# The first product of an MLP reads its tokens 32 columns apart, and rows of x and results move in one transfer a chunk

## The chip, the cores and the metric

The kernel runs on one core of one Trainium2 chip. A core has a matrix engine (TensorE, PE in the profile; its weight loads are shown as PEld), VectorE (DVE), ScalarE (ACT), GpSimd (POOL) and SyncE (SP), which here only issues DMA transfers. The engines run side by side, each through its own list of instructions in order, and wait for each other by semaphores. SBUF is the working memory with 128 partitions; PSUM takes the products of PE; DRAM holds inputs, outputs and a scratch copy of some rows. The metric is the time of one execution in microseconds on the device.

## What is computed

A linear attention whose features are products of two random projections, and behind it a layer norm with an MLP and a residual:

```python
def phi(x):                       # x: (4, 4, 1088, 32), S1, S2: (8, 32)
    a = np.einsum('rd,bhsd->bhsr', S1, x)
    b = np.einsum('rd,bhsd->bhsr', S2, x)
    return np.einsum('bhsi,bhsj->bhsij', a, b).reshape(*x.shape[:-1], 64)
q_p, k_p = (phi(q), phi(k))
kv = np.einsum('bhsf,bhsd->bhfd', k_p, v)
z = np.sum(k_p, axis=2)
num = np.einsum('bhsf,bhfd->bhsd', q_p, kv)
den = np.einsum('bhsf,bhf->bhs', q_p, z)[..., None] + 1e-06
x = (num / den)                   # then (B, S, H*D) = (4, 1088, 128)
xn = (x - mean(x)) / np.sqrt(var(x) + 1e-06) * g_ln
ch = np.maximum(xn @ w_ch1, 0.0) @ w_ch2     # 128 -> 512 -> 128
out = x + ch
```

All arithmetic is in float32. The MLP weights come as 64 bit floats and are turned into float32 on the chip.

## The kernel before

**Tokens and chunks.** Each of the four batches has 1088 tokens, 32 runs of 34: on loading, partition 32 h + i holds tokens 34 i to 34 i + 33 of head h. The MLP works on ten chunks: chunks 0 to 7 are half a batch, 512 tokens in four tiles of 128, and chunks 8 and 9 hold the remaining 64 tokens of two batches each, one tile of 128. The output of the attention stands in `xT`: features on the 128 partitions, tokens along the columns. `num_cp` copies it there from four PSUM banks, so that column 128 t + 32 r + i of a chunk (tile t, bank r) is token 34 i + 4 r + t of its batch, and 16 more in the second half. The four r of one i, sixteen neighbouring tokens with their four t, lie 32 columns apart.

**The MLP of a chunk.** The layer norm is folded into the products: the mean is taken out by the weights `w1`, and the factor 1/sqrt(var) is applied to the result, since it is positive and passes through the ReLU. `hid` is the first product: for each of four column blocks j of `w1`, the block is the weight and the 512 columns of `xT` are streamed past it, into one PSUM bank. `relu` moves that bank to `hT` in SBUF, on ACT or DVE. `sec` is the second product: for each tile t, the 128 columns of `hT` of that tile are the weights and `w2` streams past, four times, added up in PSUM. So the tokens come out on partitions, in the order in which `hid` read the columns. `fin` (DVE) or `fin_a` (ACT) with `fin_g` (POOL) scale the result and add the row of `x`; `store` writes it to DRAM.

**Rows of x.** The residual and the statistics (`st_bn`, `st_ag` on DVE, `st_pow` on POOL) need `x` with tokens on partitions, in the same order. Chunks 0, 8 and 9 get it by a transposition on PE (`row_pe`, `row_cp`). Chunks 1 to 7 go through DRAM: `row_turn` transposes blocks of 32 x 32 on DVE into `xh`, `row_wr` writes `xh` to the scratch `xd`, and `row_rd` reads it back in another arrangement, in one transfer for each r: 32 partitions, 64 KB. `store` likewise writes 32 partitions (`g` is r there), 64 KB, four times a chunk.

**Order of the work.** Nothing plans the order at run time or build time. `PROGRAM`, a text at the end of the kernel, lists all steps in one order, and each engine gets its instructions in that order; a step's letter S, A, V or G names the engine (SP, ACT, DVE, POOL) that does it, or that issues its DMA. So a transfer issued by ACT stands in ACT's list between its copies and ReLUs, and what it waits for holds up what is behind it. `fill` steps in the early part are products of ones with no use for the result.

The lines that the prediction speaks of: L232, L223, L193 are fills of constants on POOL; L382 is `sk_0`; L553 is `k_sccp` and L652 `q_den`, two reductions on DVE; L787 `row_pe`; L77 a copy on ACT; L802 `row_wr`, L808 `row_rd`; L843 `hid`, L851 `relu` on ACT, L859 `sec`; L872 `fin`, L888 `fin_g`; L893 `store`, L902 `store_r`.

Of the kernel before, what the change touches and what calls it, by code (L numbers as in the profile page):

```python
# [24 lines left out]
def kernel(  # L25
# [32 lines left out]
    dve, act, pool, pe, sp = nc.vector, nc.scalar, nc.gpsimd, nc.tensor, nc.sync  # L58
    by = {"V": dve, "A": act, "G": pool, "S": sp}
# [271 lines left out]
    w1 = const([P, DH], F32, "w1")  # L331
# [435 lines left out]
    xd = [dram.tile([P, 512 if i < 8 else P], F32, name=f"xd{i}") for i in range(10)]  # L767
# [69 lines left out]
    def ob(c):  # L837
        return obs[order.index(c) % len(obs)]

    @op  # L840
    def hid(z, c, j, t0, t1):
        a, n = P * t0, P * (t1 - t0)
        pe.matmul(banks[z][:, 0:n], w1[:, P * j : P * (j + 1)], cols(c)[:, a : a + n], start=True,  # L843
                  stop=True)

    @op
# [41 lines left out]
        by[eng].tensor_tensor(out=o, in0=o, in1=i, op=ALU.add)  # L888

    @op  # L890
    def store(eng, c, g, t0, t1):
        b, half = divmod(c, 2)
        by[eng].dma_start(  # L893
            out=bass.AP(out.tensor, out.offset + (b * S + 16 * half + 4 * g + t0) * DM,
                        [[G * DM, 32], [1, DM * (t1 - t0)]]),
            in_=ob(c)[32 * g : 32 * g + 32, DM * t0 : DM * t1],
        )

    @op
# [50 lines left out]
    k_sccp V 2; relu A C 1 2 0 4; k_val 1; k_tok 3 0 0 9; k_tok 3 1 0 9; row_rd S 1 3; q_turn 0 4;  # L950
    ld_v S 2 0; k_sum 3; q_feat 2 0 9; ld_v S 3 2; k_vcp A 1; sk_qq 3; row_rd S 1 1; st_ag 0;
    k_spr 1; q_tok 2 1 0 9; sec M 0 2; ld_v S 2 2; k_rcp A 1; q_tok 2 2 0 9; ld_v S 3 3;
    q_tok 2 0 0 9; sec O 1 2; row_rd S 1 2; q_tok 2 3 0 9; ld_v S 3 1; k_zs 3; sec M 0 3;
    q_turn 4 9; q_ac G 2 4 9; ld_vr S 3 1; st_pow 0; sec O 1 0; k_prod V 2 0 5; k_prod G 2 5 9;
    k_sc 3; fin_a M 0; num 1 0 9; sec O 1 3; num_cp A 1 1 0 4; num_cp V 1 2 4 8; num_cp A 1 3 0 4;
    num_cp V 1 2 0 4; num_cp A 1 0 0 4; row_rd A 1 0; k_sccp V 3; row_turn 2; hid N 2 3 0 4;
    num_cp A 1 3 4 8; num_r A 1; turn_h q 3 0; row_wr S 2; row_pe 8 D; hid K 2 1 0 4;
    relu A N 2 3 0 4; q_den 2 4 9; turn_h q 3 1; num_cp A 1 0 4 8; hid C 2 2 0 4; q_rec 2 4 9;
    relu A K 2 1 0 4; turn_r q 3; q_ac V 2 0 4; q_a2 G 2 4 9; row_cp A 8 D; q_den 2 0 4;
    num_cp A 1 1 4 8; sec O 1 1; relu A C 2 2 0 4; q_prod V 2 4 9; hid B 3 0 0 4; q_rec 2 0 4;  # L960
# [6 lines left out]
    st_bn 8; sec M 2 0; hid N 3 2 0 4; relu A D 8 3 0 1; relu V K 8 1 0 1; row_rd A 2 1;
    q_ac V 3 4 9; st_ag 1; relu A C 8 0 0 1; k_val 3; row_rd A 2 2; relu V A 8 2 0 1; st_pow 1;
    relu V N 3 2 0 4; q_den 3 4 9; num 2 0 9; q_rec 3 4 9; k_vcp A 3; fin_a O 1; q_a2 G 3 4 9;
    q_ac G 3 0 4; q_prod G 3 4 9; k_spr 3; num_cp V 2 1 4 8; sec O 3 2; num_cp V 2 3 4 8;  # L970
    num_cp V 2 2 0 4; num_cp A 2 3 0 4; st_ag 8; st_bn 3; num_cp A 2 2 4 8; sec O 3 0; k_rcp A 3;
    num_r V 2; sec N 8 0; st_ag 3; num_cp A 2 1 0 4; num_cp V 2 0 0 4; st_pow 3; num_cp V 2 0 4 8;
    hid C 4 2 0 4; row_turn 5; row_turn 4; row_wr S 5; sec O 3 3; fin_g G 1; q_turn 4 9;
    row_wr S 4; sec O 3 1; store S 0 0 0 4; st_bn 2; hid A 5 1 0 4; relu A C 4 2 0 4; row_rd A 5 3;
    q_den 3 0 4; hid C 4 0 0 4; row_rd S 4 1; q_rec 3 0 4; store A 0 1 0 4; relu V A 5 1 0 4;
    store S 0 2 0 4; store A 0 3 0 4; hid D 5 3 0 4; st_ag 2; row_rd S 5 2; fin_a O 3;
    q_a2 V 3 0 4; st_pow 2; store S 1 3 0 4; q_prod V 3 0 4; hid B 4 3 0 4; row_rd S 5 0;
    relu A C 4 0 0 4; hid A 4 1 0 4; relu A D 5 3 0 4; st_pow 8; q_turn 0 4; row_rd S 5 1;
# [6 lines left out]
    num_cp V 3 0 0 4; row_wr A 7; row_cp V 9 N; sec K 5 3; row_turn 6; store A 3 0 0 4;
    row_rd A 4 0; st_bn 5; sec K 4 0; store A 1 1 0 4; st_ag 5; sec K 4 2; row_rd S 7 0; st_pow 5;
    row_wr S 6; hid N 6 2 0 4; st_bn 4; hid B 6 0 0 4; relu A N 6 2 0 4; st_ag 4; store A 2 3 0 4;
    hid C 6 1 0 4; st_pow 4; relu A B 6 0 0 4; row_rd S 6 2; store_r A 8 1; hid A 6 3 0 4;
    relu V C 6 1 0 4; row_rd S 6 1; fin K 4 0; sec N 5 0; row_rd S 6 0; fin D 4 3; row_rd S 7 3;
    sec M 5 2; row_rd S 7 1; fin N 5 0; fin O 4 1; row_rd S 7 2; st_bn 9; row_rd A 6 3;  # L990
    hid C 7 3 0 4; st_ag 9; fin K 4 2; relu V A 6 3 0 4; sec B 5 1; fin M 5 2; sec N 6 0;
    relu A C 7 3 0 4; sec O 6 1; relu V D 9 0 0 1; fin B 5 1; fin K 5 3; hid A 9 2 0 1; st_bn 6;
    store S 5 3 0 4; hid D 7 2 0 4; relu A A 9 2 0 1; store S 4 0 0 4; relu V M 9 3 0 1;
    hid K 7 0 0 4; store S 5 1 0 4; st_ag 6; relu A D 7 2 0 4; st_bn 7; st_pow 6; store_r S 8 0;
    store A 5 0 0 4; hid B 7 1 0 4; store S 3 3 0 4; relu A K 7 0 0 4; st_ag 7; store S 4 2 0 4;
    store A 4 1 0 4; sec D 6 3; st_pow 9; store S 3 1 0 4; store A 4 3 0 4; relu A B 7 1 0 4;
    sec A 6 2; st_pow 7; relu A O 9 1 0 1; fin N 6 0; sec A 7 0; fin O 6 1; fin D 6 3; sec C 7 3;
# [38 lines left out]
```

## Time and profile before

| | us |
|---|---|
| median of three timed runs | 103.03 |
| lowest and highest of them | 102.94, 105.31 |
| the profiled execution, its own time | 102.81 |
| span of the profiled execution | 100.9 |

The span runs from the first to the last event of the profile; the execution's own time also takes in what lies around it.

The page of the profile has the span in 40 equal slices, each digit the busy share of one slice in tenths. In most slices PE is above nine tenths, while DVE, ACT and POOL come and go:

```profile
PE   5988999999999999999999999999999999999960
DVE  2878989789999599699089549999559079661630
ACT  2863754979700720755513353029640030253000
POOL 7115998999588926912999189809920540057000
DMA  2989999893008760030023220346146445054242
```

In rows of groups, a line such as L843 is followed by the engine, the operation, what it writes and reads, the shapes, the count, the busy time in all and the mean of one, and then the idle time of the engine before these instructions with what ended it. In the chain of waits, each step is what released the next one, back from the last instruction; "x2" counts records. A float32 product on PE shows as two records, one for each pass.

### The profile page before, as it was taken

How to read it: one execution, taken by the hardware profiler on the slowest of the kernel's cores; microseconds unless marked ns; L12 is line 12 of the kernel's file. 1: busy time of each engine (PE TensorE's matmuls, PEld its weight loads, DVE VectorE, ACT ScalarE, POOL GpSimd, SP SyncE). 2: the span in 40 equal slices, each digit the busy share in tenths (PEclk: the TensorE clock that was granted, in tenths of full speed). 3: DMA queues.
4: the chain of work that ended last, by engine and by line, in shares of the span. 5: the costliest groups of instructions: out<-in, count | busy, mean ns of one | idle time of the engine just before them, and what ended most of it. 6: DMA issues, size and time to landing. Idle time of an engine off the chain costs nothing.

```text
span 100.9 us, 3433 instructions
## 1 busy us (share of the span) xinstructions
PE 95.3 (94%) x1355; PEld 68.7 (68%) x1355; DVE 74.0 (73%) x239; ACT 41.3 (41%) x119; POOL 58.4 (58%) x83
## 2 busy tenths in 40 slices
PE   5988999999999999999999999999999999999960
PEld 5765668656656779656588669854469758959950
DVE  2878989789999599699089549999559079661630
ACT  2863754979700720755513353029640030253000
POOL 7115998999588926912999189809920540057000
PEclk9999999999999999999999999999999999999999
DMA  2989999893008760030023220346146445054242
GB/s 76 272 293 389 353 370 275 272 218 88 3 6 301 212 164 3 6 130 0 6 107 106 47 59 0 109 153 187 55 107 204 143 122 148 1 115 132 77 119 64
DMA packets 12367, 13.85 MB, mean 137 GB/s; under 512 B 2880, under 2 KB 8768, under 8 KB 12352
## 3 DMA queue, kind: packets, MB, share of 16 engines
q1 hardware_dynamic: 9968, 11.67, 38.8%
q10 hardware_dynamic: 2384, 1.97, 6.7%
q8 instruction: 10, 0.16, 0.7%
q14 instruction: 5, 0.04, 0.2%
HBM read 9.57 MB, written 4.06 MB: 135 GB/s over the span
## 4 chain that ended last, share of the span: by engine, by line
PE 78%; DMA 5%; POOL 5%; DVE 2%; ACT 2%; SPq 2%; issue 1%; ACTq 0%; POOLq 0%
PE bankO L859 8%; PE bankM L859 8%; DMA w_raw<-in_moe_w_ch_dram 5%; PE bankN L843 5%; PE bankK L560 5%; PE bankC L843 4%; PE bankK L843 4%; PE bankK L859 4%; PE bankB L843 3%; PE bankA L843 3%; PE bankD L843 3%; PE bankM L250 3%; PE bankA L859 3%; PE bankN L859 3%; POOL ob L888 2%; PE bankA L735 2%
## 5 line engine op out<-in xcount | busy, mean ns | idle before, releaser
L82 POOL TENSOR_TENSOR kp<-kf 128x1024 f32<-128x1024 f32 (+4 forms) x9 | 15.9, 1779 | 0.1
L827 POOL TENSOR_SCALAR va<-mv 128x4 f32<-128x4 f32 (+1 forms) x10 | 2.3, 228 | 18.2 <-DVE mv L822 17.7
L82 POOL TENSOR_TENSOR qp<-a,fq 128x1280 f32<-128x1280 f32 (+1 forms) x5 | 11.1, 2219 | 0.2
L859 PEld LDWEIGHTS bankO<-w,hT 128*128 128x128 f32 x80 | 9.7, 192 | 1.9 <-issue 1.9
L829 POOL TENSOR_TENSOR rstd<-va,mhalf 128x4 f32<-128x4 f32 (+1 forms) x10 | 10.3, 1034 | 0.8
L859 PE MATMUL bankO<-w,hT 128*128 128x128 f32 x80 | 10.4, 277 | 0.0
L859 PEld LDWEIGHTS bankM<-w,hT 128*128 128x128 f32 x72 | 9.0, 192 | 1.9 <-issue 1.9
L677 DVE STREAM_TRANSPOSE qpT<-qp 128x1280 f32<-128x1280 f32 (+1 forms) x7 | 9.6, 1365 | 0.0
L250 PE MATMUL bankM<-ones 128*128 128x256 f32 (+1 forms) x28 | 8.3, 440 | 1.2 <-DVE top L180 1.2
L859 PE MATMUL bankM<-w,hT 128*128 128x128 f32 x72 | 9.3, 275 | 0.0
L816 DVE BATCH_NORM_STATS2 st<-x 128x6 f32<-128x128 f32 x32 | 6.7, 272 | 2.5 <-issue 2.5
L250 PEld LDWEIGHTS bankM<-ones 128*128 128x128 f32 x28 | 5.7, 241 | 2.5 <-DVE top L180 1.2
L851 ACT ACTIVATE hT<-bankC 128x512 f32<-128x512 f32 (+1 forms) x6 | 3.3, 551 | 8.3 <-PE bankB L859 4.7
L843 PE MATMUL bankC<-xT,w 128*128 128x512 f32 x12 | 6.1, 592 | 0.0
L843 PE MATMUL bankN<-xT,w 128*128 128x512 f32 (+1 forms) x14 | 6.1, 516 | 0.0
L851 ACT ACTIVATE hT<-bankN 128x256 f32<-128x256 f32 (+1 forms) x6 | 3.0, 498 | 7.2 <-PE bankN L843 7.2
L82 POOL TENSOR_TENSOR a<-fq,rden 128x160 f32<-128x160 f32 (+1 forms) x6 | 2.8, 463 | 5.2 <-DVE rden L659 4.8
L560 PEld LDWEIGHTS bankK<-kp,vn 128*32 128x32 f32 x288 | 4.2, 110 | 2.3 <-issue 1.1
L851 ACT ACTIVATE hT<-bankK 128x512 f32<-128x512 f32 (+1 forms) x6 | 3.1, 522 | 6.2 <-PE bankK L843 5.3
L457 DVE STREAM_TRANSPOSE qT<-qn 128x512 f32<-128x512 f32 x8 | 5.5, 687 | 0.0
L843 PE MATMUL bankK<-xT,w 128*128 128x512 f32 (+1 forms) x12 | 5.4, 530 | 0.0
L735 PE MATMUL bankD<-qpT,kvr 32*32 32x288 f32 (+1 forms) x64 | 5.2, 386 | 0.0
(235 smaller groups left out, 255.2 us busy)
## 6 DMA issues: line engine op xcount, KB each, us to landing
kn<-in_k_dram SPq DMA_DIRECT2D x3, 544.0 KB, 6.2
qn<-in_q_dram SPq DMA_DIRECT2D x3, 544.0 KB, 6.4
vn<-in_v_dram SPq DMA_DIRECT2D x12, 128.0 KB, 4.5
xd<-xh SPq DMA_DIRECT2D x5, 256.0 KB, 2.6
x<-xd SPq DMA_DIRECT2D x20, 64.0 KB, 2.0
out_dram<-ob SPq DMA_DIRECT2D x19, 64.0 KB, 1.7
out_dram<-ob ACTq DMA_DIRECT2D x13, 64.0 KB, 1.9
w_raw<-in_moe_w_ch_dram SPq DMA_DIRECT2D x2, 256.0 KB, 4.0
```

The source lines that it names most:

```text
L82: by[eng].tensor_tensor(out=o, in0=a, in1=b, op=ALU.mult)
L250: pe.matmul(M[0][:, 0:w], ones[:, 0:P], ones[:, 0:w], start=True, stop=True)
L457: dve.transpose(_ap(dst[b % 2], 0, P, P * 4 * half, [[32, 4], [P, 4], [1, 32]]), src[b][:, 512 * half : 512 * half + 512],)
L560: pe.matmul(KV[D * h : D * h + D, 0:F], vn[b][:, TW * h + D * u : TW * h + D * (u + 1)], kp[:, H * F * u + F * h : H * F * u + F * (h + 1) ...
L677: dve.transpose(_ap(qpT, 0, P, 32 * u0, [[32, u1 - u0], [TW, 8], [1, 32]]), qp[:, H * F * u0 : H * F * u1])
L735: pe.matmul(X[r][D * h : D * h + D, o : o + w], kvr[b % 2][rows, DM * f + D * h : DM * f + D * h + D], qpT[rows, c : c + w], start=(f == 0 ...
L816: dve.bn_stats(out=sts[slot(c)][:, 6 * t : 6 * t + 6], in_=row_ap(c, t))
L827: pool.tensor_scalar(out=vas[slot(c)][:, 0:n], in0=_ap(mvs[slot(c)], 0, P, 1, [[2, n]]), scalar1=1e-6, scalar2=None, op0=ALU.add)
L829: pool.tensor_tensor(out=rstds[slot(c)][:, 0:n], in0=vas[slot(c)][:, 0:n], in1=mhalf[:, 0:n], op=ALU.pow)
L843: pe.matmul(banks[z][:, 0:n], w1[:, P * j : P * (j + 1)], cols(c)[:, a : a + n], start=True, stop=True)
L851: act.activation(o, i, AF.Relu)
L859: pe.matmul(banks[z][:, DM * t : DM * (t + 1)], h[:, 512 * j + P * t : 512 * j + P * (t + 1)], w2[:, DM * j : DM * (j + 1)], start=(j == 0 ...
```

## The change

`hid` reads the columns of chunks 1 to 7 in another order: within each tile of 128 it takes the columns 0, 32, 64, 96, then 1, 33, 65, 97, and so on, by an access pattern with a step of 32 floats. Since the tokens come out of `sec` in that order, the four r of one i lie on four neighbouring partitions. `row_rd` then reads a chunk's rows with one pattern over 128 partitions, and `store` can write a chunk with one transfer. Chunk 0, whose rows come by PE, keeps its order and its four stores.

```diff
+    woven_chunks = set(range(1, 8))
...
     @op
     def row_rd(eng, c, r):
         w = D * tiles(c)
-        by[eng].dma_start(
-            out=_ap(rows_of(c), 32 * r, 32, 0, [[w, H], [1, w]]),
-            in_=bass.AP(xd[c].tensor, xd[c].offset + w * r, [[P // 32 * w, 32], [P * w, H], [1, w]]),
-        )
+        dst, src = _ap(rows_of(c), 0, P, 0, [[w, H], [1, w]]), [[w, P], [P * w, H], [1, w]]
+        if c > 7:
+            dst = _ap(rows_of(c), 32 * r, 32, 0, [[w, H], [1, w]])
+            src = [[P // 32 * w, 32]] + src[1:]
+        by[eng].dma_start(out=dst, in_=bass.AP(xd[c].tensor, xd[c].offset + w * r, src))
...
+    def woven(y, c, o, t0, t1):
+        if c not in woven_chunks:
+            return y[:, o + P * t0 : o + P * t1]
+        return _ap(y, 0, P, o + P * t0, [[P, t1 - t0], [1, 32], [32, 4]][t1 - t0 == 1 :])
+
     @op
     def hid(z, c, j, t0, t1):
-        a, n = P * t0, P * (t1 - t0)
-        pe.matmul(banks[z][:, 0:n], w1[:, P * j : P * (j + 1)], cols(c)[:, a : a + n], start=True,
+        n = P * (t1 - t0)
+        pe.matmul(banks[z][:, 0:n], w1[:, P * j : P * (j + 1)], woven(cols(c), c, 0, t0, t1), start=True,
                   stop=True)
...
-    def store(eng, c, g, t0, t1):
+    def store(eng, c, t0, t1, g=None):
         b, half = divmod(c, 2)
+        if g is not None:
+            by[eng].dma_start(
+                out=bass.AP(out.tensor, out.offset + (b * S + 16 * half + 4 * g + t0) * DM,
+                            [[G * DM, 32], [1, DM * (t1 - t0)]]),
+                in_=ob(c)[32 * g : 32 * g + 32, DM * t0 : DM * t1],
+            )
+            return
         by[eng].dma_start(
-            out=bass.AP(out.tensor, out.offset + (b * S + 16 * half + 4 * g + t0) * DM,
-                        [[G * DM, 32], [1, DM * (t1 - t0)]]),
-            in_=ob(c)[32 * g : 32 * g + 32, DM * t0 : DM * t1],
+            out=bass.AP(out.tensor, out.offset + (b * S + 16 * half + t0) * DM,
+                        [[G * DM, 32], [4 * DM, 4], [1, DM * (t1 - t0)]]),
+            in_=ob(c)[:, DM * t0 : DM * t1],
         )
```

In `PROGRAM` the four `row_rd` of a chunk become one, at the place of the first, issued by SP for all chunks; the four `store` of chunks 1 to 5 become one, at the place of the first, on SP; chunks 6 and 7 are stored in two halves of two tiles each, one by SP and one by ACT. The four stores of chunk 0 are all on SP. The step `sk_0`, whose result no step reads, is left out. All other steps stay in their order. Some places of it:

```diff
-    q_dir 0 4 O; q_tok 0 0 4 9; sk_0; q_tok 0 3 4 9; ld_vr S 1 1; q_tok 0 2 4 9; c_vpad 2;
+    q_dir 0 4 O; q_tok 0 0 4 9; q_tok 0 3 4 9; ld_vr S 1 1; q_tok 0 2 4 9; c_vpad 2;
...
-    row_rd A 2 3; sec M 2 1; q_tok 3 1 0 9; q_tok 3 2 0 9; k_prod G 3 5 9; hid K 8 1 0 1;
-    hid B 3 3 0 4; q_turn 4 9; k_rcp A 2; row_rd S 3 3; row_rd A 3 2; sec M 2 2; row_rd S 3 1;
+    k_spr 2; q_tok 3 0 0 9; row_rd S 2 0; sec M 2 1; q_tok 3 1 0 9; q_tok 3 2 0 9; k_prod G 3 5 9;
+    hid K 8 1 0 1; hid B 3 3 0 4; q_turn 4 9; k_rcp A 2; row_rd S 3 0; sec M 2 2; relu A B 3 3 0 4;
...
-    hid K 5 0 0 4; relu V O 5 2 0 4; fin_g G 2; store A 3 2 0 4; num 3 0 9; relu A K 5 0 0 4;
-    store S 2 2 0 4; store A 2 1 0 4; store S 1 0 0 4; sec O 4 1; num_cp A 3 3 0 4;
+    fin_g G 2; store S 3 0 4; num 3 0 9; relu A K 5 0 0 4; store S 2 0 4; sec O 4 1;
+    num_cp A 3 3 0 4; num_cp V 3 1 0 4; num_r A 3; fin N 8 0; num_cp A 3 3 4 8; num_cp A 3 1 4 8;
...
-    fin A 6 2; fin A 7 0; store S 6 2 0 4; store A 6 1 0 4; sec B 7 1; store S 6 3 0 4; fin C 7 3;
-    store S 6 0 0 4; sec K 7 2; store S 5 2 0 4; fin B 7 1; sec A 9 0; fin K 7 2; store S 7 0 0 4;
-    store A 7 2 0 4; store S 7 1 0 4; store A 7 3 0 4; fin A 9 0; store_r S 9 0; store_r A 9 1;
+    sec A 7 0; fin O 6 1; fin D 6 3; sec C 7 3; fin A 6 2; fin A 7 0; store S 6 0 2; store A 6 2 4;
+    sec B 7 1; fin C 7 3; sec K 7 2; fin B 7 1; sec A 9 0; fin K 7 2; store S 7 0 2; store A 7 2 4;
+    fin A 9 0; store_r S 9 0; store_r A 9 1;
```

More of the change, by code (lines that the diff above doesn't have):

```diff
@@ L949 @@
     turn_h q 2 1; relu A D 1 0 0 4; k_sc 2; k_feat 3 0 9; relu A N 0 3 2 4; q_prod G 1 4 9;
[L950 to L960, printed above, removed]
@@ L967 @@
[L967 to L978, printed above, removed]
@@ L985 @@
[L985 to L996, printed above, removed]
@@ L997 @@
-    sec A 6 2; st_pow 7; relu A O 9 1 0 1; fin N 6 0; sec A 7 0; fin O 6 1; fin D 6 3; sec C 7 3;
-    fin A 6 2; fin A 7 0; store S 6 2 0 4; store A 6 1 0 4; sec B 7 1; store S 6 3 0 4; fin C 7 3;
-    store S 6 0 0 4; sec K 7 2; store S 5 2 0 4; fin B 7 1; sec A 9 0; fin K 7 2; store S 7 0 0 4;
-    store A 7 2 0 4; store S 7 1 0 4; store A 7 3 0 4; fin A 9 0; store_r S 9 0; store_r A 9 1;
+    k_sccp V 2; relu A C 1 2 0 4; k_val 1; k_tok 3 0 0 9; k_tok 3 1 0 9; row_rd S 1 0; q_turn 0 4;
+    ld_v S 2 0; k_sum 3; q_feat 2 0 9; ld_v S 3 2; k_vcp A 1; sk_qq 3; st_ag 0; k_spr 1;
@@ new lines @@
+    q_tok 2 1 0 9; sec M 0 2; ld_v S 2 2; k_rcp A 1; q_tok 2 2 0 9; ld_v S 3 3; q_tok 2 0 0 9;
+    sec O 1 2; q_tok 2 3 0 9; ld_v S 3 1; k_zs 3; sec M 0 3; q_turn 4 9; q_ac G 2 4 9; ld_vr S 3 1;
+    st_pow 0; sec O 1 0; k_prod V 2 0 5; k_prod G 2 5 9; k_sc 3; fin_a M 0; num 1 0 9; sec O 1 3;
+    num_cp A 1 1 0 4; num_cp V 1 2 4 8; num_cp A 1 3 0 4; num_cp V 1 2 0 4; num_cp A 1 0 0 4;
+    k_sccp V 3; row_turn 2; hid N 2 3 0 4; num_cp A 1 3 4 8; num_r A 1; turn_h q 3 0; row_wr S 2;
+    row_pe 8 D; hid K 2 1 0 4; relu A N 2 3 0 4; q_den 2 4 9; turn_h q 3 1; num_cp A 1 0 4 8;
@@ new lines @@
+    hid C 2 2 0 4; q_rec 2 4 9; relu A K 2 1 0 4; turn_r q 3; q_ac V 2 0 4; q_a2 G 2 4 9;
+    row_cp A 8 D; q_den 2 0 4; num_cp A 1 1 4 8; sec O 1 1; relu A C 2 2 0 4; q_prod V 2 4 9;
+    hid B 3 0 0 4; q_rec 2 0 4; hid A 2 0 0 4; row_turn 3; relu A B 3 0 0 4; q_a2 G 2 0 4;
+    q_prod G 2 0 4; k_val 2; relu A A 2 0 0 4; q_feat 3 0 9; k_vcp A 2; row_wr A 3; fin_g G 0;
+    k_spr 2; q_tok 3 0 0 9; row_rd S 2 0; sec M 2 1; q_tok 3 1 0 9; q_tok 3 2 0 9; k_prod G 3 5 9;
+    hid K 8 1 0 1; hid B 3 3 0 4; q_turn 4 9; k_rcp A 2; row_rd S 3 0; sec M 2 2; relu A B 3 3 0 4;
@@ new lines @@
+    q_tok 3 3 0 9; k_prod G 3 0 5; hid A 8 2 0 1; q_turn 0 4; hid C 8 0 0 1; hid D 8 3 0 1;
+    hid N 3 1 0 4; st_bn 1; sec M 2 3; relu A N 3 1 0 4; st_bn 8; sec M 2 0; hid N 3 2 0 4;
+    relu A D 8 3 0 1; relu V K 8 1 0 1; q_ac V 3 4 9; st_ag 1; relu A C 8 0 0 1; k_val 3;
+    relu V A 8 2 0 1; st_pow 1; relu V N 3 2 0 4; q_den 3 4 9; num 2 0 9; q_rec 3 4 9; k_vcp A 3;
+    fin_a O 1; q_a2 G 3 4 9; q_ac G 3 0 4; q_prod G 3 4 9; k_spr 3; num_cp V 2 1 4 8; sec O 3 2;
+    num_cp V 2 3 4 8; num_cp V 2 2 0 4; num_cp A 2 3 0 4; st_ag 8; st_bn 3; num_cp A 2 2 4 8;
@@ new lines @@
+    sec O 3 0; k_rcp A 3; num_r V 2; sec N 8 0; st_ag 3; num_cp A 2 1 0 4; num_cp V 2 0 0 4;
+    st_pow 3; num_cp V 2 0 4 8; hid C 4 2 0 4; row_turn 5; row_turn 4; row_wr S 5; sec O 3 3;
+    fin_g G 1; q_turn 4 9; row_wr S 4; sec O 3 1; store S 0 0 4 0; st_bn 2; hid A 5 1 0 4;
+    relu A C 4 2 0 4; row_rd S 5 0; q_den 3 0 4; hid C 4 0 0 4; row_rd S 4 0; q_rec 3 0 4;
+    store S 0 0 4 1; relu V A 5 1 0 4; store S 0 0 4 2; store S 0 0 4 3; hid D 5 3 0 4; st_ag 2;
+    fin_a O 3; q_a2 V 3 0 4; st_pow 2; store S 1 0 4; q_prod V 3 0 4; hid B 4 3 0 4;
@@ new lines @@
+    relu A C 4 0 0 4; hid A 4 1 0 4; relu A D 5 3 0 4; st_pow 8; q_turn 0 4; fin_a M 2;
+    hid O 5 2 0 4; fin_g G 3; relu V A 4 1 0 4; relu A B 4 3 0 4; hid K 5 0 0 4; relu V O 5 2 0 4;
+    fin_g G 2; store S 3 0 4; num 3 0 9; relu A K 5 0 0 4; store S 2 0 4; sec O 4 1;
+    num_cp A 3 3 0 4; num_cp V 3 1 0 4; num_r A 3; fin N 8 0; num_cp A 3 3 4 8; num_cp A 3 1 4 8;
+    num_cp V 3 2 0 4; num_cp V 3 2 4 8; hid D 9 0 0 1; hid M 9 3 0 1; num_cp V 3 0 4 8;
+    hid O 9 1 0 1; row_turn 7; row_pe 9 N; sec D 4 3; num_cp V 3 0 0 4; row_wr A 7; row_cp V 9 N;
@@ new lines @@
+    sec K 5 3; row_turn 6; st_bn 5; sec K 4 0; st_ag 5; sec K 4 2; row_rd S 7 0; st_pow 5;
+    row_wr S 6; hid N 6 2 0 4; st_bn 4; hid B 6 0 0 4; relu A N 6 2 0 4; st_ag 4; hid C 6 1 0 4;
+    st_pow 4; relu A B 6 0 0 4; row_rd S 6 0; store_r A 8 1; hid A 6 3 0 4; relu V C 6 1 0 4;
+    fin K 4 0; sec N 5 0; fin D 4 3; sec M 5 2; fin N 5 0; fin O 4 1; st_bn 9; hid C 7 3 0 4;
+    st_ag 9; fin K 4 2; relu V A 6 3 0 4; sec B 5 1; fin M 5 2; sec N 6 0; relu A C 7 3 0 4;
+    sec O 6 1; relu V D 9 0 0 1; fin B 5 1; fin K 5 3; hid A 9 2 0 1; st_bn 6; store S 5 0 4;
@@ new lines @@
+    hid D 7 2 0 4; relu A A 9 2 0 1; store S 4 0 4; relu V M 9 3 0 1; hid K 7 0 0 4; st_ag 6;
+    relu A D 7 2 0 4; st_bn 7; st_pow 6; store_r S 8 0; hid B 7 1 0 4; relu A K 7 0 0 4; st_ag 7;
+    sec D 6 3; st_pow 9; relu A B 7 1 0 4; sec A 6 2; st_pow 7; relu A O 9 1 0 1; fin N 6 0;
+    sec A 7 0; fin O 6 1; fin D 6 3; sec C 7 3; fin A 6 2; fin A 7 0; store S 6 0 2; store A 6 2 4;
+    sec B 7 1; fin C 7 3; sec K 7 2; fin B 7 1; sec A 9 0; fin K 7 2; store S 7 0 2; store A 7 2 4;
+    fin A 9 0; store_r S 9 0; store_r A 9 1;
```

8 lines of the change are left out of this document (removed).

## The prediction

> **What bounds the kernel now.** I read the busy totals first, then the chain of waits, then a table of the busy time by stages whose edges I took from that chain.
>
> ```profile
> span 100.9 us, 3433 instructions
> PE 95.3 (94%) x1355; PEld 68.7 (68%) x1355; DVE 74.0 (73%) x239; ACT 41.3 (41%) x119; POOL 58.4 (58%) x83
> ```
>
> TensorE (PE) is busy for 95.3 of 100.9 us and no other engine for more than 74.0. The table by stages tells whether the rest is spread or sits at the ends (columns after the stage: its length, then PE, PEld, DVE, ACT and POOL busy, granted clock, DMA share, GB/s):
>
> ```profile
> 0.00:8.85 8.85, 6.98 (x106) 5.19 (x106) 5.60 (x29) 4.43 (x11) 2.97 (x20) 1.00 0.74 235
> 8.85:74.54 65.69, 65.58 (x1096) 45.02 (x1096) 54.46 (x149) 32.36 (x98) 49.54 (x54) 1.00 0.44 133
> 74.54:74.93 0.39, 0.27 (x3) 0.08 (x1) 0.28 (x2) 0.39 (x4) 0.00 (x0) 1.00 0.67 137
> 74.93:97.40 22.47, 22.43 (x153) 18.41 (x153) 13.31 (x62) 4.15 (x9) 5.87 (x10) 1.00 0.43 118
> 97.40:100.90 3.50, 0.00 (x0) 0.00 (x0) 0.35 (x1) 0.00 (x0) 0.00 (x0) 0.92 0.37 94
> ```
>
> There are three parts: 8.85 us of loading, 88.55 us in which PE hardly pauses at full granted clock, and 3.50 us after its last product (the last output is finished, stored and lands). Busy could hide waiting, since the ends of matmuls are modelled, so I checked the pace in the chain of waits (start, length, what):
>
> ```profile
> 79.55 0.86 PE bankN L843 x2
> 80.41 0.86 PE bankB L843 x2
> 81.27 0.86 PE bankC L843 x2
> 82.13 0.86 PE bankA L843 x2
> 82.98 0.89 PE bankN L859 x8
> ...
> 97.40 0.35 DVE ob L872
> ```
>
> L843 is `hid`, the first product of the MLP; each call is two matmul records, 0.86 us for 512 columns, so 0.43 us a pass or 0.84 ns a column. Four calls of one chunk follow each other without a gap, and `sec` (L859) follows at once. So a cost or saving on PE goes one to one into the time, and a saving elsewhere only counts where PE waits for it.
>
> **The product read in steps.** For chunks 1 to 7 `hid` now reads the columns of `xT` in the order 0, 32, 64, 96, 1, 33 and so on: four bytes taken, 128 bytes on, where before they were adjacent. That is 7 chunks x 4 calls = 28 calls and 56 passes; chunk 0 (calls of 256 columns) and the remainder chunks 8 and 9 read as before. No PE row of this trace has such a step, so the price needs bounds from the nearest rows. One is GpSimd (POOL), which fills a tile of 36 elements at a step of 9 floats, 36 bytes, and other tiles without a step (last columns: busy in all, mean ns of one):
>
> ```profile
> L232 POOL MEMSET ac<- 128x36 f32 x2 | 0.3, 158 | 0.3 <-POOLq L1020 0.3
> L223 POOL MEMSET kT<- 128x64 f32 x2 | 0.3, 144 | 0.0
> L193 POOL MEMSET ident<- 128x128 f32 x1 | 0.2, 203 | 0.0
> L1020 POOL MEMSET const-float32-1.0<- 128x1 f32 x1 | 0.1, 98 | 0.0
> ```
>
> One element takes 98 ns, which I take as the fixed part. Contiguous elements then cost (203 - 98) / 128 = 0.82 ns or (144 - 98) / 64 = 0.72 ns; the stepped ones (158 - 98) / 36 = 1.67 ns, 2.0 to 2.3 times as much. And 0.82 ns is about the pace at which `hid` reads its columns. This row is in SBUF, where `xT` lies, but it writes, and on another engine. The other neighbour reads: VectorE (DVE) reduces 32 elements out of PSUM four at a time at a step of 8 floats, beside contiguous reductions from SBUF:
>
> ```profile
> L553 DVE TENSOR_REDUCE skq<-bankK 128x8 f32<-128x32 f32 x4 | 0.7, 180 | 0.5 <-PE bankK L545 0.5
> L652 DVE TENSOR_REDUCE den<-ac 128x16 f32<-128x144 f32 x4 | 1.2, 296 | 0.1
> L652 DVE TENSOR_REDUCE den<-ac 128x20 f32<-128x180 f32 x4 | 1.3, 317 | 0.0
> ```
>
> At 0.58 ns an element between the contiguous two, (317 - 296) / 36, 32 elements would take 296 - 112 x 0.58 = 231 ns; the stepped one takes 180. It shows no penalty, though in the other memory and with few elements under a large fixed part. So a pass costs between nothing and 1.3 times its 0.43 us more. A gain has no ground: a contiguous column already comes every 0.84 ns, and nothing here reads fewer bytes in steps. I take the stepped memset, since it is in the same memory and at the same pace without steps: twice the time, 0.43 us more for each of 56 passes, **24.1 us**; at 2.3 times it would be 31 us, at the reduction's price nothing.
>
> [...]
>
> What hides 24 us? Nothing: the chain above has these calls back to back on the bound engine. Other engines only get more slack.
>
> **The transfers.** The rows of `x` were read and the results stored in quarters:
>
> ```profile
> x<-xd SPq DMA_DIRECT2D x20, 64.0 KB, 2.0
> x<-xd ACTq DMA_DIRECT2D x8, 64.0 KB, 2.2
> out_dram<-ob SPq DMA_DIRECT2D x19, 64.0 KB, 1.7
> out_dram<-ob ACTq DMA_DIRECT2D x13, 64.0 KB, 1.9
> xd<-xh SPq DMA_DIRECT2D x5, 256.0 KB, 2.6
> out_dram<-ob ACTq DMA_DIRECT2D x2, 32.0 KB, 2.2
> ```
>
> The 28 reads become 7 of 256 KB, all on SP, and 32 stores become 13 (four for chunk 0, one each for 1 to 5, two halves each for 6 and 7), of which ACT issues two. The bytes stay. A 256 KB transfer between SBUF and DRAM took 2.6 us where a quarter took 2.0 to 2.2, so a whole chunk lands 0.4 to 0.6 us after what was its first quarter; the consumers need all four, which were issued one behind the other, so they get it no later. SP takes over what ACT issued, and its list is shorter than before, 7 reads and 11 stores against 20 and 19. Two waits are moved: SP now waits for POOL's addition to chunk 3, which ACT did, and for both chunks' rows where ACT had read a part. Queued behind them are more reads and stores, and nobody on PE asks for these at once.
>
> What ACT is spared counts where PE waits for ACT, and the table has that place, 74.54 to 74.93:
>
> ```profile
> 72.62 0.32 ACTq L893 DMA_DIRECT2D out_dram<-ob  x1
> 73.85 0.37 ACTq L893 DMA_DIRECT2D out_dram<-ob  x1
> 74.27 0.27 ACT L77 COPY xT<-bankD 128x128 f32<-128x128 f32 x1 [0.68 <-POOL ob L888]
> 74.43 0.19 ACT L77 COPY xTr<-bankC 128x32 f32<-128x32 f32 x1
> 74.93 0.30 PEld L843 LDWEIGHTS bankD<-xTr,w 128*128 128x128 f32 x2 [0.31 <-ACT xT L77]
> ```
>
> ACT stood at two stores until POOL had added chunks 3 and 2 (the wait on `ob`), the copies into `xTr` came late, and PE waited for them. With the stores on SP this goes: up to 0.39 us. What is late next is PE itself, which has the last `sec` of chunk 4 until 74.54. Elsewhere ACT waits for PE:
>
> ```profile
> ACT hT L851 <- PE bankN L843: 7.2, 3, 5.4
> L382 DVE TENSOR_TENSOR sk<-bankK,m 128x64 f32<-128x64 f32 x1 | 0.2, 188 | 0.0
> 97.78 0.54 SPq L902 DMA_DIRECT2D out_dram<-ob  x1
> ```
>
> so the other spared issues, 0.3 to 0.4 us each by the two rows above, are worth nothing. The dropped `sk_0` (L382, read by no product) frees 0.19 us of DVE in a stage where PE has filler products to run; 0 to 0.19 us, I take 0. At the end the last store is issued at 97.78, right after `fin`, before and after the change; it has the same bytes of chunk 7 ahead of it: 0, at best 0.5 us if it lands in the 1.7 us of the quickest stores instead of the 2.2 of its row.
>
> **Sum.** The profiled execution took 102.81 us, 1.91 more than its span and 0.22 below the median of the three timed runs (103.03). 102.81 + 24.1 - 0.4 = **126.5 us**.
>
> **The rivals.** [...] *A dearer step*, 2.3 times and above: 102.4 + 31 = 133 us and more; the 64 column memset is all that speaks for it. *Faster by over 2%*: this needs 2.06 us, and 0.39 + 0.19 + 0.5 = 1.1 us is all that the views offer outside PE's own work, so it would take a shortening that no row shows. That the change does not do what it says is no rival: the transfers and the product's operands are written out in the code, with no scheduler between.
>
> **How the numbers follow.** Chances: twice the time 0.45 (own range 122 to 130), partial 0.11, dearer 0.04, free 0.35, faster by over 2% 0.05. A measurement of this kernel can tell about 2% from no change, so slower by over 2% is 0.45 + 0.11 + 0.04 = 0.60, within 2% is 0.35, faster 0.05. The likeliest case gives 126.5 us. The free case is too likely to be left out, so the range goes from 101.6 to 130 us and omits the dearer step, the faster case and the edges, some 0.15.
>
> **What would show it.** In the profile of the changed kernel the two records of a `hid` call of chunks 1 to 7 should be 0.86 us apart instead of 0.43, those of chunk 0 unchanged; PE busy throughout, the stage from 8.85 us to the last product some 112 us, and ACT and POOL waiting longer for PE. Calls still of 0.86 us in the chain would make the forecast wrong and the free case right; something between them the partial one. PE's pause before the remainder's product should be gone in each case, x should be read by 7 transfers of 256 KB landing in about 2.6 us, and a pause of PE for `x` or for a store would say that the transfers do matter.

## The result, and the profile after

| | before | after |
|---|---|---|
| median of all executions, us (6 each) | 103.34 | 127.97 |
| lowest and highest | 102.94, 106.67 | 127.31, 130.15 |
| the profiled execution | 102.81 | 127.31 |
| its span | 100.9 | 125.5 |

The ratio of after to before is 1.238, with a 95% interval of 1.233 to 1.244. (Here and below the ratios leave out executions that ran over 1.5% longer than the fastest of the same kernel, which the medians hold; so a ratio need not be that of the medians.)

The busy totals of the changed kernel, from its page:

```profile
span 125.5 us, 3363 instructions
PE 119.6 (95%) x1355; PEld 69.5 (55%) x1355; DVE 73.9 (59%) x238; ACT 41.3 (33%) x119; POOL 58.5 (47%) x83
```

The span grew by 24.6 us and PE's busy time by 24.3, for the same 1355 records. The totals of DVE, ACT and POOL moved by 0.1 us at most: they do the same work and idle longer. The table by stages, with the middle one from the first stage's end to just behind PE's last product (length, then PE, PEld, DVE, ACT and POOL busy, granted clock, DMA share, GB/s):

```profile
0.00:8.85 8.85, 7.16 (x108) 5.45 (x108) 6.23 (x30) 4.46 (x11) 3.65 (x26) 1.00 0.76 239
8.85:121.77 112.92, 112.47 (x1249) 64.02 (x1248) 67.64 (x209) 36.85 (x108) 54.81 (x59) 1.00 0.34 102
121.77:125.50 3.73, 0.00 (x0) 0.00 (x0) 0.05 (x1) 0.00 (x0) 0.00 (x0) 0.84 0.20 55
```

PE fills the middle stage but for 0.45 us, of which 0.30 lie behind its last product (the last `fin`, which waits for that product, starts at 121.47). The granted clock is full. So hardly anything keeps PE waiting: it works longer. The chain of waits says at what (start, length, what; the lines of the code have moved by eight, so L851 is now `hid`, L867 `sec` and L880 `fin`):

```profile
59.31 0.22 PE bankK L851 x2
...
91.10 1.09 PE bankO L867 x8
92.19 0.22 PE bankD L851 x2
...
96.54 1.74 PE bankN L851 x2
98.28 1.75 PE bankB L851 x2
100.03 1.75 PE bankC L851 x2
101.77 1.75 PE bankA L851 x2
103.52 0.89 PE bankN L867 x8
...
121.47 0.35 DVE ob L880
```

Four products of one chunk that follow each other take 103.52 - 96.54 = 6.98 us, 1.745 us each. Before, the same four took 82.98 - 79.55 = 3.43 us, 0.857 each. A remainder's product of 128 columns, which still reads adjacent columns, takes 0.22 us, and `sec` takes its 0.89 us as before. So only the stepped product became slower: by 0.888 us x 28 calls = **24.9 us**, which is the whole loss. The rows at 91.10 and 92.19 answer to PE's pause of 0.39 us in the kernel before: it is gone.

The DMA issues of the page (KB each, median us to landing) and two rows of the waits (in all, times, longest):

```profile
x<-xd SPq DMA_DIRECT2D x7, 256.0 KB, 3.0
...
out_dram<-ob SPq DMA_DIRECT2D x5, 256.0 KB, 2.4
```

```profile
POOL va L830 <- DVE mv L825: 31.8, 4, 12.5
ACT hT L859 <- PE bankK L851: 15.3, 4, 8.3
ACT hT L859 <- PE bankN L851: 11.1, 3, 6.4
```

The seven large reads land in 3.0 us, and no row of PE's waits names one. ACT's wait for the products of bank N grew from 7.2 to 11.1 us, POOL's wait for `mv` from 17.7 to 31.8, and that is slack of engines that are not the bound.

### The profile page after: what moved, and what is told of

It is laid out like the page before. It is cut to its first block, busy times and chain, and to the rows that moved or that the text cites. A ratio compares the mean times of both kernels' runs of the same rounds, so it can differ in the third digit from the quotient of the medians.

```text
span 125.5 us, 3363 instructions
## 1 busy us (share of the span) xinstructions
PE 119.6 (95%) x1355; PEld 69.5 (55%) x1355; DVE 73.9 (59%) x238; ACT 41.3 (33%) x119; POOL 58.5 (47%) x83
## 4 chain that ended last, share of the span: by engine, by line
PE 90%; DMA 3%; DVE 1%; ACT 1%; SPq 1%; issue 1%; ACTq 0%
PE bankC L851 9%; PE bankO L867 7%; PE bankB L851 7%; PE bankN L851 7%; PE bankK L851 7%; PE bankM L867 6%; PE bankA L851 6%; PE bankD L851 5%; PE bankK L560 4%; PE bankO L851 3%; DMA kn<-in_k_dram 3%; PE bankK L867 3%; PE bankM L250 3%; PE bankA L735 3%; PE bankA L867 2%; PE bankN L867 2%
## 5 line engine op out<-in xcount | busy, mean ns | idle before, releaser
L830 POOL TENSOR_SCALAR va<-mv 128x4 f32<-128x4 f32 (+1 forms) x10 | 2.3, 229 | 32.3 <-DVE mv L825 31.8
L867 PEld LDWEIGHTS bankM<-w,hT 128*128 128x128 f32 x72 | 9.1, 193 | 5.3 <-issue 5.3
L867 PEld LDWEIGHTS bankO<-w,hT 128*128 128x128 f32 x80 | 9.8, 192 | 3.6 <-issue 3.6
L851 PE MATMUL bankC<-xT,w 128*128 128x512 f32 x12 | 11.5, 1045 | 0.0
L867 PE MATMUL bankO<-w,hT 128*128 128x128 f32 x80 | 10.5, 278 | 0.0
L851 PE MATMUL bankN<-xT,w 128*128 128x512 f32 (+1 forms) x14 | 9.6, 772 | 0.0
L851 PE MATMUL bankB<-xT,w 128*128 128x512 f32 x10 | 9.6, 1046 | 0.0
L867 PE MATMUL bankM<-w,hT 128*128 128x128 f32 x72 | 9.4, 276 | 0.0
L851 PE MATMUL bankK<-xT,w 128*128 128x512 f32 (+1 forms) x12 | 8.9, 831 | 0.0
L851 PE MATMUL bankA<-xT,w 128*128 128x512 f32 x8 | 7.7, 1047 | 0.0
L859 ACT ACTIVATE hT<-bankN 128x256 f32<-128x256 f32 (+1 forms) x6 | 3.0, 502 | 11.1 <-PE bankN L851 11.1
L851 PE MATMUL bankD<-xT,w 128*128 128x512 f32 (+1 forms) x8 | 6.3, 878 | 0.0
```

The lines of the kernel that those rows point to most:

```text
L830: pool.tensor_scalar(out=vas[slot(c)][:, 0:n], in0=_ap(mvs[slot(c)], 0, P, 1, [[2, n]]), scalar1=1e-6, scalar2=None, op0=ALU.add)
L851: pe.matmul(banks[z][:, 0:n], w1[:, P * j : P * (j + 1)], woven(cols(c), c, 0, t0, t1), start=True, stop=True)
L859: act.activation(o, i, AF.Relu)
L867: pe.matmul(banks[z][:, DM * t : DM * (t + 1)], h[:, 512 * j + P * t : 512 * j + P * (t + 1)], w2[:, DM * j : DM * (j + 1)], start=(j == 0 ...
```

## The experiments

The open questions after the result were three. Is it the step alone, and if so what about the step: the short runs, the long jumps, or the number of 16-byte stretches of `xT` that the columns fall on? Where did the transfers' 0.4 us go? And is there a place where the order can be changed at no cost?

### One part without the other

**The transfers alone.** The changed kernel with `hid` reading adjacent columns everywhere:

```diff
-    woven_chunks = set(range(1, 8))
+    woven_chunks = set()
```

> The changed kernel with its transfers and without the stepped read: hid takes the columns of every chunk side by side again, so the tokens of chunks 1 to 7 come out in another order than the rows of x that are added to them. Theory (the read carries the whole loss, and the transfers are worth the saved wait of 0.4 us): 102.4 to 102.9 us beside 103.3 for the kernel before, PE's pause before the remainder's product gone. Rival (merging the transfers costs something, hidden so far behind the slower PE): more than 103.5 us, with a pause of PE that ends on a transfer.

Measured in 12 executions: ratio to before 0.9998, interval 0.995 to 1.004. The chain of waits of this kernel:

```profile
73.64 1.09 PE bankO L867 x8
74.73 0.22 PE bankD L851 x2
...
79.09 0.86 PE bankN L851 x2
...
96.93 0.35 DVE ob L880
```

The products are at 0.86 us again, and there is no pause ahead of the remainder's product: `sec` ends at 73.64 + 1.09 = 74.73, where the product starts. From the first `hid` to the end of the last `fin` it took 75.57 us against 75.97 before, so 0.40 us were saved, as forecast. But the span is 101.0 us, no less than the 100.9 of before. The stretch behind the last `fin` is 101.0 - (96.93 + 0.35) = 3.7 us, where before it is 100.9 - (97.40 + 0.35) = 3.15: the gain is given back at the end. More on that below.

**The step alone.** The kernel before, all its transfers as they were, with the stepped read in chunks 1 to 7:

```diff
-        pe.matmul(banks[z][:, 0:n], w1[:, P * j : P * (j + 1)], cols(c)[:, a : a + n], start=True,
+        pe.matmul(banks[z][:, 0:n], w1[:, P * j : P * (j + 1)], (_ap(cols(c), 0, P, a, [[P, t1 - t0], [1, 32], [32, 4]]) if c in through_dram
+                  else cols(c)[:, a : a + n]), start=True,
                   stop=True)
```

> The kernel before with its quarter transfers, and only hid of chunks 1 to 7 reads at a step of 32 columns (the order of the tokens is again not that of the rows). Theory: each of the 28 products takes 1.74 us as in the changed kernel, 28 x 0.886 = 24.8 us more, about 128 us. Rival (part of the loss comes from the transfers): clearly below 127 us.

Measured: 127.32 us for the profiled one of two executions (the other took 129.46), span 125.4, within 0.1 us of the changed kernel. Its chain of waits (here L860 is `sec`):

```profile
88.27 1.74 PE bankK L843 x2
...
91.55 1.09 PE bankO L860 x8
92.64 0.22 PE bankD L843 x2
...
121.91 0.35 DVE ob L873
```

So the step carries the loss by itself. The rows in the middle hold something that the prediction had not seen: here too PE goes from `sec` (91.55 + 1.09 = 92.64) to the remainder's product without a pause, though ACT still issues the two stores that caused it. With PE slower, ACT has time for them: it issues them at 85.12 and 90.11 us and has its copies into `xTr` done at 92.07. So the saved wait that the prediction took off comes with either part of the change.

### What it is about the step

Four kernels, all built on the changed one, differ only in the pattern that `hid` reads (and so in the order of the tokens). Its free dimensions are lists of [step, count] in floats, outermost first. A line is here and in the expectations a stretch of 16 bytes on a partition of `xT`, four neighbouring columns. That the price goes by lines was an assumption of the author's ahead of these runs; the table below has what they show of it.

Step of 8 bytes, so that two columns of each 16 bytes are read in a row:

```diff
-        return _ap(y, 0, P, o + P * t0, [[P, t1 - t0], [1, 32], [32, 4]][t1 - t0 == 1 :])
+        return _ap(y, 0, P, o + P * t0, [[P, t1 - t0], [1, 2], [2, 64]][t1 - t0 == 1 :])
```

> The changed kernel with hid reading at a step of 2 columns (8 bytes: all even columns of a tile, then all odd ones) in place of 32; the order of the tokens is another one. Theory by lines of 16 bytes: two reads fall on each line, so no price, 0.86 us a product and about 102.7 us. Rival (any step other than one column costs): 1.74 us a product and about 128 us.

Step of 16 bytes, a short distance too, but with one column of each 16 bytes:

```diff
-        return _ap(y, 0, P, o + P * t0, [[P, t1 - t0], [1, 32], [32, 4]][t1 - t0 == 1 :])
+        return _ap(y, 0, P, o + P * t0, [[P, t1 - t0], [1, 4], [4, 32]][t1 - t0 == 1 :])
```

> The same with a step of 4 columns (16 bytes), 32 columns in a run before the next starts. Theory by lines: each read falls on a new line, the full price as at a step of 32, 1.74 us a product and about 128 us. Rival (the price lies in the long jump of 128 bytes or in the short run of four columns, after which the pattern starts again): clearly less, 0.86 us a product and about 102.7 us in the limit.

Pairs of neighbours, then on by the 128 bytes of the change:

```diff
-        return _ap(y, 0, P, o + P * t0, [[P, t1 - t0], [1, 32], [32, 4]][t1 - t0 == 1 :])
+        return _ap(y, 0, P, o, [[2, 16], [32, 16], [1, 2]])
```

> The changed kernel with hid reading pairs of neighbouring columns, the next pair 32 columns on (8 bytes adjacent, then a jump of 128 bytes); the order of the tokens is another one. Theory by lines of 16 bytes: two reads fall on a line before the next line, so 0.86 to 0.90 us a product and 102.8 to 104 us. Rival (jumps of 128 bytes cost by themselves, once a pair): halfway, about 1.3 us a product and 115 us.

Step of 12 bytes, so that 16 bytes hold 1.33 of the columns read:

```diff
-        return _ap(y, 0, P, o + P * t0, [[P, t1 - t0], [1, 32], [32, 4]][t1 - t0 == 1 :])
+        return _ap(y, 0, P, o, [[43, 4], [3, P]])
```

> The changed kernel with hid reading at a step of 3 columns (12 bytes), four runs of 128 that start 43 columns apart; a few columns are read twice and others not, so the output is not the reference's. Of four reads in a row two share a line and two have a line to themselves. Theory (a line costs as much as two columns, however many of the two are taken): 6 column times for 4 columns, 1.5 x 0.86 = 1.29 us a product, 102.8 + 28 x 0.43 = 115 us. Rival (a threshold: steps under 16 bytes are free): 0.86 to 0.90 us and 103 to 104 us. Other rival (any pattern that is not two to a line pays in full): 1.74 us and 127 us.

From the chains of waits, products that follow each other without a gap; first that of 8 bytes, then 16 bytes, the pairs, and 12 bytes:

```profile
81.03 0.90 PE bankN L851 x2
...
83.73 0.90 PE bankA L851 x2
```

```profile
81.18 1.80 PE bankC L851 x2
...
90.18 1.80 PE bankK L851 x2
```

```profile
78.97 0.87 PE bankN L851 x2
...
81.56 0.87 PE bankA L851 x2
```

```profile
76.36 1.36 PE bankD L851 x2
...
81.80 1.36 PE bankK L851 x2
```

There are three products between the starts in the first and third fence, five in the second, four in the fourth, so a product takes 2.70 / 3 = 0.90, 9.00 / 5 = 1.80, 2.59 / 3 = 0.863 and 5.44 / 4 = 1.36 us. The times of the kernels:

| read | lines of 16 bytes per column | us a product | us of the kernel |
|---|---|---|---|
| adjacent (the transfers alone) | 0.25 | 0.86 | 102.86 (median of 12) |
| pairs, jumps of 128 bytes | 0.5 | 0.86 | 102.75 (one) |
| step of 8 bytes | 0.5 | 0.90 | 104.95 (median of 2) |
| step of 12 bytes | 0.75 | 1.36 | 117.86 (one) |
| step of 16 bytes | 1 | 1.80 | 129.67 (median of 2) |
| step of 128 bytes (the change) | 1 | 1.745 | 127.97 (median of 6) |

The second column is the step over 16 bytes, at most 1 (for adjacent columns four share a line, for pairs two). The time follows it: 1.80 us a line and column gives 0.75 x 1.80 = 1.35 and 0.5 x 1.80 = 0.90, against 1.36 and 0.90 measured, down to the 0.86 us that adjacent columns and pairs both take. (The steps of 12 and 16 bytes came out a little dearer than the 1.29 and 1.74 us expected.) The rivals fall. Long jumps cost nothing: the pairs jump as far as the change does and take 0.863 us, where adjacent columns take 0.86. Nor does it matter that the innermost run is of one column: at a step of 8 bytes it is, and costs 0.04 us (0.90 against 0.86). Nor does it help to come back to a line soon: the change returns to each line after four columns (0, 32, 64, 96, then 1) and takes 1.745 us a product, as for a new line each time. The size of 16 bytes stands in the table as well: from a step of 8 bytes to one of 16 the product doubled, 0.90 to 1.80 us, and at 128 bytes it took no more, 1.745.

Of the 2.4 us by which the span with the step of 8 bytes is longer than before (103.3 against 100.9), the products explain 28 x 0.043 = 1.2. Its first `hid` also began later, at 22.84 us against 21.78, though the edit touches nothing ahead of it. The pause of 0.4 us that is gone and an end that is 0.6 us longer (below) nearly cancel. Its ratio, 1.017, has a wide interval (1.005 to 1.029).

### Where the transfers' gain went

Behind the last `fin` all kernels do the same: the last outputs are stored and land, and SP waits for them. Yet the stretch from the end of the last `fin` to the end of the span was 3.1 us in some profiles and 3.7 in others. The output itself landed as before: the last store lands 2.15 to 2.20 us behind the last `fin` in all profiles. What differs is SP. It has five waits at the end, and in the profiles with 3.7 us it stands for 0.44 us between the second and the third (with the transfers alone from 99.57 to 100.01), although the semaphores of the third were satisfied at 97.6. The rest, some 0.2 us, is the order of the waits: there the wait for the last store is the first of the five, so that the others come behind it; in the profiles with 3.0 to 3.1 us it is the third or the last. Two of the three kernels here test whether that hangs on SP's list of instructions, and one asks for the saved wait alone.

**Rows of x in quarters again, all on SP**: the transfers alone, as above, with 21 more reads in SP's list:

```diff
-        dst, src = _ap(rows_of(c), 0, P, 0, [[w, H], [1, w]]), [[w, P], [P * w, H], [1, w]]
...
-        by[eng].dma_start(out=dst, in_=bass.AP(xd[c].tensor, xd[c].offset + w * r, src))
+        for r in (0, 1, 2, 3):
+            by[eng].dma_start(
+                out=_ap(rows_of(c), 32 * r, 32, 0, [[w, H], [1, w]]),
+                in_=bass.AP(xd[c].tensor, xd[c].offset + w * r, [[P // 32 * w, 32], [P * w, H], [1, w]]),
+            )
```

> The kernel with plain reads and merged stores, the rows of x read in quarters again but all by SP: 21 more transfers in SP's list (the order of the tokens is not that of the rows). The plain-read kernel lost at the end what it won in the pause of PE: from the end of the last output's DVE instruction to the end of the span 3.74 us against 3.15 us before, with a pause of 0.44 us of SP between two of its last waits whose transfers had landed long before. Theory (the pause hangs on the place in SP's list, not on the stores): with a longer list it is elsewhere, 3.15 to 3.3 us at the end and 102.4 us. Rival (it comes with the merged stores of the last chunks): 3.7 us and 102.9 us.

Measured: ratio 0.989, interval 0.983 to 0.996. The four quarters instead of one transfer cost nothing, and the end is short again: 100.0 - (96.70 + 0.35) = 2.95 us. The transfers from 97 to 101.5 us, first of the kernel with one transfer a chunk, then of this one: the rate in 40 equal slices of 0.1125 us, and the queues by kind (packets, MB, share of 16 engines):

```profile
GB/s 319 110 0 0 0 64 319 337 319 128 0 0 0 64 155 92 123 132 18 0 0 0 0 0 0 0 0 0 0 0 0 0 73 0 0 0 0 0 0 0
...
q10 hardware_dynamic: 224, 0.16, 12.4%
q1 hardware_dynamic: 143, 0.08, 6.8%
q14 instruction: 1, 0.01, 0.7%
```

```profile
GB/s 0 0 0 82 346 319 337 82 0 0 0 64 173 78 150 105 14 0 0 0 0 0 0 0 0 0 0 0 0 0 0 0 0 0 0 0 0 0 0 0
...
q10 hardware_dynamic: 224, 0.16, 12.3%
q1 hardware_dynamic: 81, 0.03, 3.5%
```

The first has a packet on the queue of the kind "instruction" at 97 + 32 x 0.1125 = 100.6 us, long after the last bytes of the output (the 19th slice, up to 99.1 us); the second does not. The profile's page has five such packets on this queue in both kernels (0.04 MB, so 8 KB each); the fifth falls at another place, 74.9 us in the second.

**Stores in halves**: the kernel with the reordering ReLU (below) with the stores of chunks 1 to 5 in two halves, so only five more transfers in SP's list (that of chunk 3 is shown, the others go alike):

```diff
-    store S 3 0 4;
+    store S 3 0 2; store S 3 2 4;
...
```

> The kernel with the reordering in relu and merged reads, and the stores of chunks 1 to 5 in two halves of two tiles each: only five transfers more in SP's list. Theory (SP's pause of 0.44 us among its last waits hangs on their place in its list): the pause leaves the last waits, the end falls from 3.74 us to 3.0 to 3.3 us, about 0.5 us less than with whole stores, a ratio near 0.990. Rival (it needs the reads in quarters): 3.7 us at the end, ratio 0.996 as measured with whole stores.

Measured: ratio 0.996, interval 0.991 to 1.001, where 0.990 was expected: as with whole stores, so the gain at the end shows in the profile and not in the times. The span is 101.6 us, since its first `hid` began late (23.00 us), but the end is short: 101.6 - (98.22 + 0.35) = 3.0 us. Five more transfers on SP are enough. Over all 13 profiles of this study the two things go together without exception: in the seven kernels with the short list of the change (after, the transfers alone, the four patterns, the reordering ReLU) one such packet of 8 KB falls within the last 3 us and the end takes 3.7 us; in the six with more transfers on SP there is none, and it takes 3.0 to 3.1. The packet is not what SP stands for: it begins 0.6 to 0.9 us after SP's pause has ended (at 100.64 us with the transfers alone, where SP goes on at 100.01). At most the two mark the same place in SP's list; what SP stands for is open.

**The two stores alone**: the kernel before with the two stores at which ACT had stood given to SP:

```diff
-    store A 3 2 0 4;
+    store S 3 2 0 4;
...
-    store A 2 1 0 4;
+    store S 2 1 0 4;
```

> The kernel before with only two steps changed: the store of a quarter of chunk 3 and the store of a quarter of chunk 2 that stood in ACT's list between its ReLUs are issued by SP. Theory (PE's pause of 0.39 us before the remainder's product came from ACT waiting at these two): the pause is gone, the end stays at 3.1 us, 0.4 us less, a ratio of 0.996. Rival (something else is late there, such as POOL's addition itself): pause and time as before.

Measured: ratio 0.995, interval 0.990 to 1.000. Its chain of waits shows the pause gone, 75.55 + 1.09 = 76.64:

```profile
75.55 1.09 PE bankO L859 x8
76.64 0.22 PE bankD L843 x2
```

and the end is at 102.3 - (98.84 + 0.35) = 3.1 us. Yet from the first `hid` to the last `fin` only 0.08 us less passed than before in this profile (of an execution of 104.43 us). The attention step `num` of batch 3 (L735), which comes ahead of these rows, began in its place, 50.35 us behind the first `hid` against 50.34, but ended 0.3 us later: its products in bank B waited 0.2 us until ACT's ReLU had emptied that bank. This ReLU began 0.35 us later than before; ahead of it in ACT's list stand a read of x and two stores, and the read was issued 0.7 us later than before. What held the read was not found. With the transfers alone ACT issues none of the three, and the 0.40 us are saved in full. The gain of half a per cent is at the edge of what was measured.

### Another place for the new order

The four columns can be interleaved one step later, where the product leaves PSUM: `hid` reads adjacent columns and `relu` reads its bank at a step of 32 floats and writes `hT` adjacent. Everything behind `relu` is that of the change.

```diff
-    woven_chunks = set(range(1, 8))
+    woven_chunks = set()
...
         o, i = hT[turn_of(c)][:, a : a + n], banks[z][:, 0:n]
+        if 1 <= c <= 7:
+            o = _ap(hT[turn_of(c)], 0, P, a, [[P, t1 - t0], [4, 32], [1, 4]])
+            i = _ap(banks[z], 0, P, 0, [[P, t1 - t0], [1, 32], [32, 4]])
```

> The changed kernel with the reordering moved off PE: hid reads side by side, and relu of chunks 1 to 7 reads its PSUM bank at a step of 32 floats and writes hT contiguously, on ACT and DVE. The output is the reference's. Theory: PE is the bound and the ReLUs have room, so at worst a ReLU of 0.60 us doubles in its 0.43 us of columns to 1.03 us beside PE, and the time is that of the transfers alone, 102.4 to 103.5 us, about 1.00 of the kernel before. Rival (ACT's ReLUs come late for the second product, PE waits for them): over 105 us with waits of PE for hT.

Measured in 12 executions: ratio 0.996, interval 0.991 to 1.002. The groups of ReLUs, first of the kernel before, then of this one (busy in all, mean ns of one | idle before and its releasers):

```profile
L851 ACT ACTIVATE hT<-bankK 128x512 f32<-128x512 f32 x4 | 2.4, 598 | 6.2 <-PE bankK L843 5.3 <-POOL ob L888 0.9
L853 DVE TENSOR_SCALAR hT<-bankA 128x512 f32<-128x512 f32 x3 | 2.0, 675 | 0.2 <-PE bankA L843 0.2
```

```profile
L862 ACT ACTIVATE hT<-bankK 128x512 f32<-128x512 f32 x4 | 2.4, 597 | 5.5 <-PE bankK L851 5.5
L864 DVE TENSOR_SCALAR hT<-bankA 128x512 f32<-128x512 f32 x3 | 2.0, 674 | 0.2 <-PE bankA L851 0.2
```

The same ReLU takes 597 ns with the step and 598 without on ACT, 674 and 675 on DVE. Out of PSUM the step cost neither of them anything here, and the products are at 0.86 us.

**With the reads in quarters of 32 partitions on SP**, which lengthen SP's list:

```diff
-        dst, src = _ap(rows_of(c), 0, P, 0, [[w, H], [1, w]]), [[w, P], [P * w, H], [1, w]]
...
-        by[eng].dma_start(out=dst, in_=bass.AP(xd[c].tensor, xd[c].offset + w * r, src))
+        for r in (0, 1, 2, 3):
+            by[eng].dma_start(
+                out=_ap(rows_of(c), 32 * r, 32, 0, [[w, H], [1, w]]),
+                in_=bass.AP(xd[c].tensor, xd[c].offset + 32 * r * w, [[w, 32], [P * w, H], [1, w]]),
+            )
```

> The kernel with the reordering in relu (output of the reference) and the rows of x read in quarters of 32 partitions, all by SP, so that SP's list is as long as in the run with quarter reads. Theory: PE stays at 0.86 us a product, its pause is gone, and the end is 3.0 us as with the longer list: 101.9 to 102.4 us, a ratio of 0.989 to 0.995, below the kernel before. Rival (the gain of the quarter reads needed the order of tokens that it had): 1.00.

Measured: ratio 0.994, interval 0.989 to 0.998; end 102.3 - (98.97 + 0.35) = 3.0 us. It keeps the change's order of tokens and its undivided stores, and is 0.6% faster than the kernel before. The two moved stores alone gave 0.5%, with as many transfers as before, so a gain from fewer transfers as such is not shown.

## Why the prediction came out right

**The product read in steps** was the step that decided, and its size was right within 4%: 24.1 us forecast, 24.9 measured. A column cost 1.745 us / 1024 = 1.70 ns, where the stepped memset of POOL had 1.67; the factor was 2.04 for the 2.0 that the prediction took. The term was a little small because of that factor alone: the count of 28 calls and the claim that nothing hides them held, since the span grew by nearly the whole of it. The stated range, 101.6 to 130 us, held the free read as well; what came true is the likeliest case in it.

That the memset was the better neighbour than the reduction on DVE turned out true. The reduction read PSUM, and the ReLUs show stepped reads of PSUM to be free in this kernel on DVE and ACT (674 ns against 675, 597 against 598). The prediction gave "the other memory" as a reservation; whether it is the memory or the engine that matters is open, since no run has DVE or ACT read SBUF at such a step. That the two prices of POOL and PE agree so closely (POOL's step was 36 bytes, and it writes) was not taken apart, and may be luck.

**The free read** (0.35) fell by the first row of a product, and **the partial price** (0.11) with it: 1.74 us, where the free read would have left the 0.86 of adjacent columns. No run shows either at this step, so none shows the free case that the lower end of the range, 101.6 us, stands for. A partial price exists at another step: 1.36 us for 12 bytes.

**The transfers** were the step that went wrong, by half a microsecond. The pause of 0.39 us did go, as the term of -0.4 us said. But it goes with the step alone as well as with the transfers alone, so in this change it can't be put down to the transfers, as the prediction did. And the end of the kernel, taken as 0 with a best case of 0.5 us gained, lost 0.6: the landing of the last store was the only thing that the prediction looked at there, and it stayed; SP's own list was not asked. The two nearly cancel. In the profiles the sum is +24.9 for the products, -0.4 for the pause, -0.3 for an earlier first `hid` (21.48 against 21.78 us, chunk 0's, ahead of every stepped product) and +0.6 at the end, 24.8 us, where the span shows 24.6.

**The landing of x** was forecast at about 2.6 us from the writes of the same size, and took 3.0. **The dropped** `sk_0` and ACT's spared issues were taken as nothing. No run isolates them. With the transfers alone, the 0.40 us saved behind the first `hid` are the pause and leave nothing for ACT's issues; `sk_0`, at 13.0 us, lies ahead of it, where the start of the first `hid` varies by more than its 0.19 us.

Of the signs that were named, the doubled products, the stage of 112 us (8.85 to 121.47, 112.6), the missing pause and the longer waits of ACT and POOL are all in the rows above.

## What to carry to other kernels

When a matmul in float32 streams its operand from SBUF at a step, count the 16-byte lines that it touches per column, and measure one such product: here up to one line for two columns cost 5% at most (0.86 and 0.90 us against 0.86), one line for each column doubled the time (1.745 and 1.80 us), and jumps of 128 bytes between lines were free (0.863 us for the pairs). If an order has to be changed, try it where an engine with slack reads PSUM; here the ReLUs did it at no cost (597 ns against 598 on ACT). And before fewer transfers are paid for with work on the bound engine, find the wait that they would end; here all of them together were worth 0.4 us, and the end of the kernel took it back.

## What the runs showed of the hardware

- In the six patterns the price of PE's float32 read went by lines of 16 bytes, as the table above has it: at a line for each column 1.70 to 1.76 ns a column (1.745 and 1.80 us over 1024) against 0.84 ns for an adjacent column. A step of 16 bytes is a little dearer than one of 128 (1.80 against 1.745 us), for which no reason was looked for.
- ACT and DVE read PSUM at a step of 128 bytes as fast as adjacent columns: 597 and 674 ns for a ReLU of 128x512, against 598 and 675.
- A longer list of SP went with a shorter end: with 5 or 21 more transfers on SP, the stretch behind the last `fin` was 3.0 us instead of 3.7 in three of three profiles. Of the ratios only that of the quarter reads (0.989 against 0.9998) shows it.
- The place where the first `hid` starts varied from 21.35 to 23.75 us between profiles, with the code ahead of it unchanged but for `sk_0`. Differences under 2 us between single profiles were therefore read from the stretch behind it, not from the span.
